# The last microseconds of a decode block: result columns split 304/208 between ScalarE and VectorE, and the last row's weight loads in front of its waiting matmul

## Chip, core and metric

One core of a Trainium2 chip. The metric is the device time of one execution in microseconds. A profile gives a span that is shorter than the time of the execution it was taken in (398.6 us for one of 401.14). The repeats and the experiments ran in groups on the chips numbered 3, 13 and 15; a ratio compares only executions of one group.

## The reference

One decode step. Attention with a cache of 65,536 keys in 4 groups of heads, and an MLP, added into one row of 1024 values. Only the ends matter here:

```python
return x + _A_ref(xn, A_k_cache, A_v_cache, A_wq, A_wo) + _B_ref(xn, B_w1, B_w2, B_w3, B_w4)
# _A_ref ends with      ... .reshape(B, Sq, Hq * Dh) @ wo
# _B_ref ends with      x1 + _gelu(_layernorm(x1, axis=-1) @ w3) @ w4        w4: 3584 x 1024
```

## The kernel before

All weights and the cache (170 MB) stream through three 8 MB buffers on one DMA queue. The last weight, w4, arrives in pieces of 8, 11, 5, 2 and 1 row blocks (of 128 rows each; a 28th block comes in small transfers and is computed earlier). "Row" below is such a block: 128 inputs times 1024 outputs. Rows 19 to 26 are computed "narrow": four 32-column tiles of the TensorE array work side by side, each on a quarter of the 1024 outputs. Quarters 0 and 1 go to one tile in PSUM, the memory that TensorE's results go to (half h = 0), 2 and 3 to another (h = 1). ScalarE copies the first half out, VectorE the second.

```python
W4_PIECES = (8, 11, 5, 2, 1)
WHOLE = 27
NARROW = 8
# ... all that comes before the tail is cut
    quarters = [ps_M.tile([P, 512], F32, name="pm_r", tag="pm") for _ in range(2)]
    sums = [ogpool.tile([64, 256], F32, name="sums_a", tag="og"), ppool.tile([64, 256], F32, name="sums_b", tag="p")]
    # ... inject(h, ...) is a matmul into quarters[h][64*h : 64*h+64, 0:256]; cut
    nc.scalar.copy(out=sums[0][:], in_=psB[0:64, 0:256])             # sums of the rows done so far
    nc.vector.tensor_copy(out=sums[1][:], in_=psB[0:64, 256:512])

    def narrow_rows(lo, hi):
        wt = st.tiles["w4"]
        for c in range(lo, hi):
            for h in range(2):
                for j in range(2):
                    q = 2 * h + j
                    nc.tensor.matmul(quarters[h][32 * q:32 * q + 32, 0:256], lhsT=hT[:, c:c + 1].to_broadcast([P, 32]),
                                     rhs=wt[:, D * c + 512 * j + 256 * h:D * c + 512 * j + 256 * (h + 1)], ...)

    with tc.issue_after(inject(0, ident_f[0:64, 0:64], sums[0][:], False)):   # half 0: old sums by TensorE
        narrow_rows(WHOLE - NARROW, WHOLE)

    out_t = ogpool.tile([64, 2, 256], BF16, name="out_t", tag="og")
    nc.scalar.copy(out=out_t[:, 0, :], in_=quarters[0][0:64, 0:256])
    nc.vector.tensor_tensor(out=out_t[:, 1, :], in0=quarters[1][64:128, 0:256], in1=sums[1][:], op=ALU.add)
    nc.scalar.dma_start(out=out[0, 0, :].rearrange("(j n) -> j n", j=2), in_=...)   # the store, from ScalarE's queue
```

Of the kernel before, what the change touches and what calls it, by code (L numbers as in the profile page):

```python
# [8 lines left out]
BF16 = mybir.dt.bfloat16  # L9
F32 = mybir.dt.float32  # L10
ACTF = mybir.ActivationFunctionType
ALU = mybir.AluOpType
# [3 lines left out]
P = 128  # L16
# [7 lines left out]
WHOLE = 27  # L24
FIRST = 6
NARROW = 8


def keep_loaded_weights(nc):




    for function in nc.m.functions:
        for block in function.blocks:
            held, kept = {}, []
            pe = [i for i in block.instructions if i.engine == mybir.EngineType.PE]
            user = dict(zip((i.name for i in pe), pe[1:]))
            for i in block.instructions:
                if i.engine == mybir.EngineType.PE:  # L40
                    if i.opcode == "Ldweights":
                        what = (i.tile_size, str(i.ins[0]))
                        waits = [j for j in (i, user[i.name]) if j.sync_info is not None and j.sync_info.on_wait]
                        if waits:
                            held.clear()
                        elif held.get(i.tile_position) == what and i.sync_info is None:
                            continue
                        if any(size != i.tile_size for size, _ in held.values()):
                            held.clear()
                        held[i.tile_position] = what  # L50
                    elif i.opcode != "Matmult" or i.ldweights is not False:
                        held.clear()
                kept.append(i)
            block.instructions = kept


# [41 lines left out]
def kernel(  # L98
# [13 lines left out]
):  # L112
    nc = tc.nc
    nc.at_finalize(keep_loaded_weights)
    nc.at_finalize(lead_with_the_first_load)
    nc.at_finalize(close_on_the_store)
    D = A_x.shape[-1]
# [19 lines left out]
    ppool = ctx.enter_context(tc.tile_pool(name="psb", bufs=1))  # L137
    ogpool = ctx.enter_context(tc.tile_pool(name="og", bufs=2))
# [82 lines left out]
    for b in range(2):  # L221
        nc.gpsimd.tensor_copy(
            out=spread[:, 2 * b:2 * b + 2, :].rearrange("p r (a i) -> p r a i", a=4),
            in_=ident_f[:, 64 * b:64 * b + 64].rearrange("p (i r) -> p r i", r=2).unsqueeze(2).to_broadcast([P, 2, 4, 32]))
# [8 lines left out]
    psB = ps_B.tile([P, 512], F32, name="psB")  # L233
# [6 lines left out]
    for a in range(4):  # L240
        nc.vector.transpose(out=x_t[32 * a:32 * a + 32].rearrange("p c j -> p (c j)"),  # L241
                            in_=x_row[:, 256 * a:256 * (a + 1)].rearrange("p (i c) -> p c i", c=DC))
# [3 lines left out]
    def layernorm(src, tag):  # L246
# [39 lines left out]
                          in_=sel8[:].unsqueeze(2).to_broadcast([P, 8, 16]))  # L286
# [49 lines left out]
    hT = const.tile([P, WHOLE + LEFT], BF16, name="hT")  # L336
# [119 lines left out]
    tail = {}  # L456
# [41 lines left out]
    def compute_w4(lo, hi):  # L498
# [3 lines that stand above are left out]
                mm = row_acc(j, hT[:, c:c + 1], wt[:, D * c + 512 * j:D * c + 512 * (j + 1)])  # L502
        return mm.ins
# [24 lines left out]
    with tc.issue_after(filled):  # L528
        projected = project(HKV - 1)
    quarters = [ps_M.tile([P, 512], F32, name="pm_r", tag="pm") for _ in range(2)]  # L530
    sums = [ogpool.tile([64, 256], F32, name="sums_a", tag="og"), ppool.tile([64, 256], F32, name="sums_b", tag="p")]
    pick = small.tile([64, 2, 32], F32, name="pick", tag="msk")
    nc.vector.tensor_copy(out=pick[:], in_=ident_f[0:64, 0:64].rearrange("p (j r) -> p j r", r=32)[:, :, 0:1].to_broadcast([64, 2, 32]))

    def inject(h, lhsT, rows, start):
        return nc.tensor.matmul(quarters[h][64 * h:64 * h + 64, 0:256], lhsT=lhsT, rhs=rows, start=start,
                                stop=False, tile_position=(0, 64 * h), skip_group_check=True).ins

    with tc.issue_after(projected):
        for h in range(2):  # L540
            begun = inject(h, pick[:].rearrange("p j r -> p (j r)"), tail["o"][0:64, 256 * h:256 * (h + 1)], True)
    with tc.issue_after(begun):
        compute_w4(early, WHOLE - NARROW)
    nc.scalar.copy(out=sums[0][:], in_=psB[0:64, 0:256])
    nc.vector.tensor_copy(out=sums[1][:], in_=psB[0:64, 256:512])

    def narrow_rows(lo, hi):
        wt = st.tiles["w4"]
        for c in range(lo, hi):
            for h in range(2):  # L550
                for j in range(2):
                    q = 2 * h + j
                    nc.tensor.matmul(quarters[h][32 * q:32 * q + 32, 0:256], lhsT=hT[:, c:c + 1].to_broadcast([P, 32]),
                                     rhs=wt[:, D * c + 512 * j + 256 * h:D * c + 512 * j + 256 * (h + 1)], start=False, stop=False,
                                     tile_position=(0, 32 * q), skip_group_check=True)

    with tc.issue_after(inject(0, ident_f[0:64, 0:64], sums[0][:], False)):
        narrow_rows(WHOLE - NARROW, WHOLE)

    out_t = ogpool.tile([64, 2, 256], BF16, name="out_t", tag="og")  # L560
    nc.scalar.copy(out=out_t[:, 0, :], in_=quarters[0][0:64, 0:256])
    nc.vector.tensor_tensor(out=out_t[:, 1, :], in0=quarters[1][64:128, 0:256], in1=sums[1][:], op=ALU.add)
    nc.scalar.dma_start(out=out[0, 0, :].rearrange("(j n) -> j n", j=2),
                        in_=out_t[31:33].rearrange("p h n -> p (h n)"))

# [1 line left out]
_INS = ['A_x', 'A_k_cache', 'A_v_cache', 'A_wq', 'A_wo', 'B_x', 'B_w1', 'B_w2', 'B_w3', 'B_w4']  # L567
# [26 lines left out]
```

## Time and profile before

| | before |
|---|---|
| time, first three executions | 400.79, 400.72, 401.16 us |
| profiled span | 398.6 us |
| last weight landed | 396.45 us |
| from there to the end of the span | 2.166 us |
| store issued, before the end of the span | 1.256 us |

The lines of the profile are shown and read in the prediction. In these lines PE is TensorE, PEld its weight loads, DVE VectorE, ACT ScalarE and ACTq ScalarE's queue; L553 is a line of the kernel, and the brackets give the engine's idle time before the instruction and what ended it.

### The profile page before, as it was taken

Reading aid. Unit: us, or ns where it says so; the run is one execution under the profiler, and the core shown is the slowest. Engines: PE = TensorE matmul, PEld = TensorE weight load, DVE = VectorE, ACT = ScalarE, POOL = GpSimd, SP = SyncE. Lnnn points to the kernel's source line nnn. Section 1 sums busy time; section 2 is a strip of 40 time slices with the busy share of each in tenths; the row PEclk is TensorE's granted clock in tenths of the full one; section 3 lists DMA queues with packets and bytes.
Section 4 is the critical chain, followed back from the end, with each engine's and each line's share of the span. In section 5 each row is a group of like instructions: output and inputs, shape, how many; then the busy total and the mean of one; then the engine's idle time right before and its main releaser. Section 6 shows DMA issues by size and latency. Waiting matters only on the chain.

```text
span 398.6 us, 2623 instructions
## 1 busy us (share of the span) xinstructions
PE 230.2 (58%) x1372; PEld 45.2 (11%) x862; DVE 211.5 (53%) x162; ACT 27.8 (7%) x36; POOL 10.0 (3%) x38
## 2 busy tenths in 40 slices
PE   0272970591569247834964297429553946394986
PEld 0210010000200010011001100101010102010142
DVE  0602010965196559643963696269449932894141
ACT  1002010003000200020002000200110020002000
POOL 2100000000000000000000000000000000002000
PEclk9998896697659686966895679678966986599999
DMA  9998999999999999999999999999999999999996
GB/s 421 421 443 382 439 441 480 434 427 421 416 428 427 434 460 442 427 427 421 427 429 427 467 434 434 423 421 427 441 429 441 454 427 388 418 455 431 409 427 260
DMA packets 4310, 170.03 MB, mean 427 GB/s; under 512 B 457, under 2 KB 459, under 8 KB 844
## 3 DMA queue, kind: packets, MB, share of 16 engines
q1 hardware_dynamic: 4294, 169.87, 98.9%
q8 instruction: 9, 0.15, 0.2%
q14 instruction: 1, 0.01, 0.0%
q10 hardware_dynamic: 6, 0.00, 0.0%
HBM read 169.87 MB, written 0.00 MB: 426 GB/s over the span
## 4 chain that ended last, share of the span: by engine, by line
DMA 54%; DVE 21%; PE 18%; ACT 2%; another core or an unknown queue 2%; SPq 1%; POOLq 1%; issue 1%; DVEq 0%; ACTq 0%
DMA big<-in_A_k_cache_dram 41%; DVE big L387 15%; PE sc L392 11%; DMA big<-in_B_w_dram 7%; DMA big<-in_A_wq_dram 6%; PE oacc L442 4%; DVE p_sb L413 2%; DVE mx L397 2%; PE psq L307 2%; ACT p_sb L410 2%; SPq L194 1%; POOLq L589 1%; ACT L410 0%; PE pm_mx L399 0%
## 5 line engine op out<-in xcount | busy, mean ns | idle before, releaser
L392 PE MATMUL sc<-big,qdiag 128*128 128x512 bf16 x512 | 128.5, 411 | 65.8 <-DVE big L387 65.6
L387 DVE STREAM_TRANSPOSE big<-big 128x4096 f32<-128x4096 f32 x32 | 139.4, 4412 | 48.0 <-DMA big<-in_A_k_cache_dram 48.0
L442 PE MATMUL oacc<-big,p_sb 128*32 128x512 bf16 x512 | 44.0, 520 | 34.5 <-DVE p_sb L413 34.5
L397 DVE TENSOR_REDUCE mx<-sc 128x1 f32<-128x2048 f32 x8 | 18.3, 2291 | 29.7 <-PE sc L392 29.7
L392 PEld LDWEIGHTS <-qdiag 128*128 128x128 bf16 x128 | 13.1, 102 | 176.6 <-issue 145.2
L410 ACT ACTIVATE p_sb<-sc,nball 128x2048 bf16<-128x2048 f32 x8 | 15.7, 1967 | 219.4 <-DVE nball L408 219.4
L413 DVE STREAM_TRANSPOSE p_sb<-p_sb 128x2048 bf16<-128x2048 bf16 x8 | 18.5, 2311 | 18.0 <-ACT p_sb L410 18.0
L442 PEld LDWEIGHTS <-p_sb 128*32 128x32 bf16 x512 | 16.8, 126 | 59.1 <-DVE p_sb L413 35.1
L451 DVE SCALAR_TENSOR_TENSOR og<-oacc,wb,og 128x512 f32<-128x512 f32 x4 | 3.0, 750 | 28.7 <-PE oacc L442 28.7
L307 PE MATMUL psh<-big,ln_rep_b 128*32 128x512 bf16 (+1 forms) x64 | 12.4, 942 | 4.0 <-DMA big<-in_B_w_dram 4.0
L485 PE MATMUL o_acc<-big,oT 128*1 128x512 bf16 x48 | 11.9, 413 | 2.4 <-ACT p_sb L410 2.4
L399 PE MATMUL pm_mx<-ident_f,mx 128*1 128x128 f32 x8 | 2.3, 283 | 19.1 <-DVE mx L397 19.1
L307 PE MATMUL psq<-big,ln_rep_a 128*32 128x512 bf16 x64 | 8.9, 445 | 4.1 <-DMA big<-in_A_wq_dram 4.1
L348 DVE STREAM_TRANSPOSE h_row<-h_row 128x896 bf16<-128x896 bf16 x1 | 1.1, 1111 | 17.2 <-ACT h_row L347 17.2
L332 POOL COPY qdiag<-qx 32x32 bf16<-32x32 bf16 x16 | 3.2, 203 | 262.8 <-PE sc L392 246.0
L250 PE MATMUL pm_ln<-ln_rowsum_a,ones_f 128*128 128x1 f32 x2 | 0.6, 348 | 12.5 <-DVE ln_rowsum_a L248 12.5
L320 DVE CAST q_row<-psq 64x1024 bf16<-64x1024 f32 x1 | 1.2, 1217 | 11.9 <-PE psq L307 11.9
L236 PE MATMUL psB<-big,hT 128*32 128x512 bf16 x46 | 5.5, 380 | 2.6 <-DMA big<-in_B_w_dram 2.6
L241 DVE STREAM_TRANSPOSE x_t<-x_row 32x256 bf16<-32x256 bf16 x4 | 2.5, 615 | 8.1 <-DMA x_row<-in_A_x_dram 8.0
L464 PE MATMUL pm_e<-ol,sel8big 128*128 128x129 f32 x6 | 1.8, 385 | 7.9 <-DVE ol L462 7.9
L406 PE MATMUL pm_mx<-ident_f,rep 1*128 1x1 f32 x8 | 1.9, 234 | 5.0 <-DVE rep L403 5.0
L448 ACT COPY og<-oacc 128x512 f32<-128x512 f32 x4 | 2.3, 585 | 33.5 <-PE oacc L442 24.4
(112 smaller groups left out, 77.1 us busy)
## 6 DMA issues: line engine op xcount, KB each, us to landing
big<-in_A_wo_dram SPq DMA_DIRECT2D x1, 8192.0 KB
big<-in_B_w_dram SPq DMA_DIRECT2D x1, 7168.0 KB
big<-in_B_w_dram SPq DMA_DIRECT2D x3, 2048.0 KB
big<-in_B_w_dram SPq DMA_DIRECT2D x1, 2816.0 KB
big<-in_B_w_dram SPq DMA_DIRECT2D x1, 1280.0 KB
big<-in_B_w_dram SPq DMA_DIRECT2D x1, 512.0 KB
big<-in_B_w_dram SPq DMA_DIRECT2D x1, 256.0 KB
big<-in_A_k_cache_dram SPq DMA_DIRECT2D x8
```

The source lines that it names most:

```text
L194: go(out=t[i0:i0 + 4 * k:4, WHOLE * D:(WHOLE + m) * D].rearrange("e (i n) -> e i n", i=m), in_=w4_v[m0:m0 + k * m, WHOLE, :].rearrange("(i ...
L236: return nc.tensor.matmul(psB[32 * j:32 * j + 32, :], lhsT=lhsT.to_broadcast([lhsT.shape[0], 32]), rhs=rhs, start=start, stop=False, tile_ ...
L307: nc.tensor.matmul(acc[32 * q:32 * q + 32, i, 0:n], lhsT=rep[:, c, :], rhs=cols(c, i, q), start=(c == 0), stop=(c == DC - 1), tile_positio ...
L332: nc.gpsimd.tensor_copy(out=qdiag[at, LEAD:].rearrange("p (x c) -> p x c", x=4)[:, :, 32 * a:32 * a + 8], in_=qx[at, :, 8 * g:8 * g + 8])
L387: nc.vector.transpose(out=words, in_=words)
L392: nc.tensor.matmul(sc[:, e, :], lhsT=qdiag[:, c0:c0 + P], rhs=cols[:, s, e, :, b2, :, r], start=(s == 0 and b2 == 0 and r == 0), stop=(s = ...
L397: nc.vector.reduce_max(out=mx[:], in_=sc[:].rearrange("p e n -> p (e n)"), axis=AX.X)
L410: nc.scalar.activation(out=p_sb[:], in_=sc[:], func=ACTF.Exp, bias=nball[:, b:b + 1], scale=SCALE, accum_out=group["lall"][:, b:b + 1])
L413: nc.vector.transpose(out=flat, in_=flat)
L442: mm = nc.tensor.matmul(oacc[32 * q:32 * (q + 1), :], lhsT=pT[:, e, 32 * t:32 * (t + 1)], rhs=vt[:, :, e, t, :], start=(e == 0 and t < 4), ...
L485: nc.tensor.matmul(tail["rows"][0:1, h2, :], lhsT=oT[g][:, j:j + 1], rhs=wt[:, g, j, 512 * h2:512 * (h2 + 1)], start=(g == 0 and j == 0), ...
L589: with _tile.TileContext(nc) as tc:
```

## The change

The intent: in the profile before, ScalarE is faster per column (0.83 against 1.04 ns) and starts 44 ns sooner than VectorE, so it takes more of the result columns (304 against 208); and the weights of the last row, which do not depend on the late transfer, are loaded before TensorE waits for that transfer.

```diff
+CUT = (0, 304, 512)
+def load_last_row_ahead(nc):
+    # (core of it) the last eight PE instructions are four pairs of load and matmul:
+            row = pe[-8:]
+            loads, sums = row[::2], row[1::2]
+            moved = {i.name for i in loads[1:]}
+            for i in block.instructions:
+                if i.name == sums[0].name:
+                    kept += loads[1:]          # in front of the matmul that waits
+                if i.name not in moved:
+                    kept.append(i)
-    sums = [... [64, 256] ..., ... [64, 256] ...]
+    cuts = [slice(CUT[h], CUT[h + 1]) for h in range(2)]
+    sums = [... [64, CUT[1]] ..., ... [64, CUT[2] - CUT[1]] ...]
-                    nc.tensor.matmul(quarters[h][32 * q:32 * q + 32, 0:256], ...
-                                     rhs=wt[:, D * c + 512 * j + 256 * h:D * c + 512 * j + 256 * (h + 1)], ...
+                    nc.tensor.matmul(quarters[h][32 * q:32 * q + 32, cuts[h]], ...
+                                     rhs=wt[:, D * c + 512 * j + CUT[h]:D * c + 512 * j + CUT[h + 1]], ...
-    nc.scalar.copy(out=out_t[:, 0, :], in_=quarters[0][0:64, 0:256])
-    nc.vector.tensor_tensor(out=out_t[:, 1, :], in0=quarters[1][64:128, 0:256], in1=sums[1][:], op=ALU.add)
+    nc.scalar.copy(out=out_t[:, cuts[0]], in_=quarters[0][0:64, cuts[0]])
+    nc.vector.tensor_tensor(out=out_t[:, cuts[1]], in0=quarters[1][64:128, cuts[1]], in1=sums[1][:], op=ALU.add)
```

(The injections and the copies out of psB take the same cuts.)

More of the change, by code (lines that the diff above doesn't have):

```diff
@@ L53, in keep_loaded_weights @@
                 kept.append(i)
+            block.instructions = kept
+def load_last_row_ahead(nc):
+    for function in nc.m.functions:
+        for block in function.blocks:
+            pe = [i for i in block.instructions if i.engine == mybir.EngineType.PE and i.opcode in ("Ldweights", "Matmult")]
+            if len(pe) < 8:
+                continue
+            row = pe[-8:]
+            loads, sums = row[::2], row[1::2]
+            assert all(i.opcode == "Ldweights" and i.sync_info is None for i in loads)
+            assert all(i.opcode == "Matmult" and i.tile_size == (P, 32) for i in sums)
+            assert sorted(i.tile_position for i in loads) == [(0, 32 * q) for q in range(4)]
+            moved = {i.name for i in loads[1:]}
+            kept = []
+            for i in block.instructions:
[3 more added lines that the diff above has]
+                    kept.append(i)
             block.instructions = kept
@@ L114 @@
     nc.at_finalize(keep_loaded_weights)
+    nc.at_finalize(load_last_row_ahead)
     nc.at_finalize(lead_with_the_first_load)
@@ L530 @@
     quarters = [ps_M.tile([P, 512], F32, name="pm_r", tag="pm") for _ in range(2)]
-    sums = [ogpool.tile([64, 256], F32, name="sums_a", tag="og"), ppool.tile([64, 256], F32, name="sums_b", tag="p")]
+    cuts = [slice(CUT[h], CUT[h + 1]) for h in range(2)]
+    sums = [ogpool.tile([64, CUT[1]], F32, name="sums_a", tag="og"),
+            ppool.tile([64, CUT[2] - CUT[1]], F32, name="sums_b", tag="p")]
     pick = small.tile([64, 2, 32], F32, name="pick", tag="msk")
@@ L535, in inject @@
     def inject(h, lhsT, rows, start):
-        return nc.tensor.matmul(quarters[h][64 * h:64 * h + 64, 0:256], lhsT=lhsT, rhs=rows, start=start,
+        return nc.tensor.matmul(quarters[h][64 * h:64 * h + 64, cuts[h]], lhsT=lhsT, rhs=rows, start=start,
                                 stop=False, tile_position=(0, 64 * h), skip_group_check=True).ins
@@ L540 @@
         for h in range(2):
-            begun = inject(h, pick[:].rearrange("p j r -> p (j r)"), tail["o"][0:64, 256 * h:256 * (h + 1)], True)
+            begun = inject(h, pick[:].rearrange("p j r -> p (j r)"), tail["o"][0:64, cuts[h]], True)
     with tc.issue_after(begun):
         compute_w4(early, WHOLE - NARROW)
-    nc.scalar.copy(out=sums[0][:], in_=psB[0:64, 0:256])
-    nc.vector.tensor_copy(out=sums[1][:], in_=psB[0:64, 256:512])
+    nc.scalar.copy(out=sums[0][:], in_=psB[0:64, cuts[0]])
+    nc.vector.tensor_copy(out=sums[1][:], in_=psB[0:64, cuts[1]])
     def narrow_rows(lo, hi):
@@ L552, in narrow_rows @@
                     q = 2 * h + j
-                    nc.tensor.matmul(quarters[h][32 * q:32 * q + 32, 0:256], lhsT=hT[:, c:c + 1].to_broadcast([P, 32]),
-                                     rhs=wt[:, D * c + 512 * j + 256 * h:D * c + 512 * j + 256 * (h + 1)], start=False, stop=False,
+                    nc.tensor.matmul(quarters[h][32 * q:32 * q + 32, cuts[h]], lhsT=hT[:, c:c + 1].to_broadcast([P, 32]),
+                                     rhs=wt[:, D * c + 512 * j + CUT[h]:D * c + 512 * j + CUT[h + 1]], start=False, stop=False,
                                      tile_position=(0, 32 * q), skip_group_check=True)
@@ L558 @@
         narrow_rows(WHOLE - NARROW, WHOLE)
-    out_t = ogpool.tile([64, 2, 256], BF16, name="out_t", tag="og")
-    nc.scalar.copy(out=out_t[:, 0, :], in_=quarters[0][0:64, 0:256])
-    nc.vector.tensor_tensor(out=out_t[:, 1, :], in0=quarters[1][64:128, 0:256], in1=sums[1][:], op=ALU.add)
-    nc.scalar.dma_start(out=out[0, 0, :].rearrange("(j n) -> j n", j=2),
-                        in_=out_t[31:33].rearrange("p h n -> p (h n)"))
+    out_t = ogpool.tile([64, 512], BF16, name="out_t", tag="og")
+    nc.scalar.copy(out=out_t[:, cuts[0]], in_=quarters[0][0:64, cuts[0]])
+    nc.vector.tensor_tensor(out=out_t[:, cuts[1]], in0=quarters[1][64:128, cuts[1]], in1=sums[1][:], op=ALU.add)
+    nc.scalar.dma_start(out=out[0, 0, :].rearrange("(j n) -> j n", j=2), in_=out_t[31:33, :])
 _INS = ['A_x', 'A_k_cache', 'A_v_cache', 'A_wq', 'A_wo', 'B_x', 'B_w1', 'B_w2', 'B_w3', 'B_w4']
```

## The prediction

> **What bounds the kernel now.** I read the page from the top: the DMA rows first, then the chain that ended last, then the end of the timeline, because the diff touches nothing but the last stage.
>
> ```profile
> DMA  9998999999999999999999999999999999999996
> q1 hardware_dynamic: 4294, 169.87, 98.9%
> HBM read 169.87 MB, written 0.00 MB: 426 GB/s over the span
> ```
>
> The DMA row is at nine tenths in nearly every slice and only its last slice drops to six. One load queue keeps the 16 engines at 98.9% of the span. So the kernel is a stream of 169.87 MB with compute beside it; nothing done on an engine shortens it, except after the last byte. The chain of waits in order of time says the same of the end:
>
> ```profile
> 384.40 12.05 DMA big<-in_B_w_dram
> 396.45 0.04 issue
> 396.50 0.34 PE pm_r L553 x4
> 396.84 0.02 issue
> 396.86 0.42 DVE out_t L562
> ```
>
> The last piece of w4 (one row of 128) lands at 396.45 us. What follows until the span's end at 398.6 us is 2.15 us, and that is all that an engine change can shorten. The timeline of this stretch shows who does what there:
>
> ```profile
> 394.10 0.36 ACT L544 COPY sums_a<-psB 64x256 f32<-64x256 f32 x1 [26.32 <-PE psB L236]
> 394.50 0.42 DVE L545 COPY sums_b<-psB 64x256 f32<-64x256 f32 x1 [5.08 <-ACT sums_a L544]
> 394.52 0.64 PE L536 MATMUL pm_r<-sums_a,ident_f 64*64 64x256 f32 x2 [0.46 <-ACT sums_a L544]
> 395.09 1.18 PE L553 MATMUL pm_r<-big,hT 128*32 128x256 bf16 x28
> 395.87 0.20 PEld L553 LDWEIGHTS <-hT 128*32 128x32 bf16 x8 [0.23 <-issue]
> 396.50 0.29 PE L553 MATMUL pm_r<-big,hT 128*32 128x256 bf16 x4 [0.23 <-DMA big<-in_B_w_dram]
> 396.50 0.10 PEld L553 LDWEIGHTS <-hT 128*32 128x32 bf16 x3 [0.43 <-issue]
> 396.82 0.36 ACT L561 CAST out_t<-pm_r 64x256 bf16<-64x256 f32 x1 [2.35 <-PE pm_r L553]
> 396.86 0.42 DVE L562 TENSOR_TENSOR out_t<-pm_r,sums_b 64x256 bf16<-64x256 f32 x1 [1.95 <-PE pm_r L553]
> 397.36 0.26 ACTq L563 DMA_DIRECT2D out_dram<-out_t  x1
> ```
>
> Four things to see. Of the last row's four weight loads only the first runs before the wait; three are recorded after the landing, among the matmuls. ScalarE starts 44 ns before VectorE (unrounded 396.817 and 396.861). ScalarE also finishes first (365 against 425 ns): 397.182 against 397.286. The store is issued at 397.362, 76 ns after VectorE, and the remaining 1.24 us to the span's end is the store's own.
>
> The trace's semaphore records give this in ns from the start of the last row (its first matmul, t = 0, 43 ns after the landing): second matmul done at 300, ScalarE from 322 to 687, fourth matmul done at 342, VectorE from 366 to 791, store issued at 867. The second and fourth signals lie 42 ns apart, so each matmul with its load follows the one before by 21 ns, and the first was done near 279.
>
> **What the Trainium skill says.** "TensorE: Matmul & The Clock Gate", section "Single matmul latency", gives (398 + N)/2.4 ns for a warm isolated matmul: 272 ns for N = 256. My 279 agrees within 7 ns; the granted clock was 1.00 from 396.0 to 397.4 us. The same page, section "The mechanism" with its list of what overlaps, says that a weight load runs beside matmuls in flight only when their row group differs, and that packed tiles otherwise start about 4 ns apart. All four tiles here span the same 128 rows, so the in-line loads should cost; the 21 ns spacing fits this. "PSUM — Partial Sum Buffer", "PSUM bank collisions raise a hardware error", asks that two engines keep to different banks or quadrants. The trace shows ScalarE and VectorE reading the result side by side, while the copies out of psB, one bank, are serial (394.10, then 394.50). The result halves already are two full-bank tiles before the change, so the words "banks of their own" describe no new overlap. "ScalarE: Activation LUTs", "What ACT_TABLE_LOAD costs", gives 0.833 ns per column; the trace agrees: a 64x1024 cast from PSUM took 1003 ns, (1003 - 365)/768 = 0.831.
>
> **The change part by part.** The instruction order of both builds differs in the last eight PE instructions only (four loads, then four matmuls, instead of pairs) and in the widths. Counts are the same: no instruction, transfer or wait goes or comes.
>
> *Widths at the end.* ScalarE takes 304 columns: 365 + 48 x 0.831 = 405 ns. VectorE takes 208: its slope from PSUM is (1217 - 416)/768 = 1.043 ns per column (64x1024 cast against the 64x256 copy), so 425 - 50 = 375 ns. The matmuls of the first half get 48 columns more, 48/2.4 = 20 ns; those of the second half 20 ns less.
>
> *Loads ahead.* The three later loads move into idle time of PE. If spacing falls from 21 to about 4 ns, the matmuls end like this: first 279 + 20 = 299, second 303; the fourth would be done by 279 - 20 + 12 = 271 by itself, but matmuls end in order, so about 303 to 311.
>
> *Sum.* ScalarE starts 22 ns after its signal, at 325, and ends at 730. VectorE starts 24 ns after, at 327 to 335, and ends at 702 to 710. The later end is now 730 instead of 791, so 61 ns are gained. The store followed the late engine by 76 ns, of which 38 were the queue's separate wait for VectorE. That wait now ends early and only ScalarE's remains, which may save up to 36 ns more. Together 61 to 97 ns; I take 70. The landing, the row's start and the store's 1.24 us stay.
>
> *Earlier in the tail.* The copy of psB to sums_a grows by 40 ns, and the two-pass f32 injection of 304 columns by about 2 x 50 ns (its two passes start 260 ns apart for 256 columns, 1.02 ns per column). So rows 19 to 23 start near 395.23 instead of 395.09. The last of them was issued at 395.55, and PE then waited for the next piece until 395.87: 0.32 us of slack, of which 0.14 is used, plus some 20 ns for width. It is hidden. VectorE's copy of sums_b starts 40 ns later, shrinks by 50, and has nearly 2 us to spare.
>
> **The rivals.**
> (1) *The loads cost nothing*, because the queue hides them already or the spacing is the matmuls' own. Then only the widths act: second matmul done at 300 + 20 = 320, fourth near 322, ScalarE 342 to 747, VectorE 346 to 721. End 747 against 791: 44 ns. For it: the reported load and matmul starts lie 1 to 2 ns apart. Against it: the 42 ns between the two signals. Time 400.75.
> (2) *ScalarE becomes too late*: 304 columns overshoot if the loads were the whole delay of VectorE. With loads alone (256/256) the end would be at about 279 + 12 + 24 + 425 = 740, so the widths add only 10 ns to that. It is still no loss: ScalarE would have to start after 386 to end later than 791. Time 400.75 to 400.80.
> (3) *The longer injection delays the rows until a landed piece waits for PE.* For it: the slack shrinks from 0.32 to some 0.16 us. Against it: two more waits for DMA follow, the last with 0.23 us of idle PE. A landing some 0.2 us earlier in another execution would use it up, and even then only part reaches the end. Time at most 400.9.
> (4) *The stream moves more than the tail.* The three timed runs go from 400.72 to 401.16 and the profiled execution took 401.14. This scatter, 0.44 us, is six times my gain. It decides what is measured, and I expect no separable difference from few rounds.
>
> **Range and chances.** 400.79 - 0.07 = 400.72 us, 0.02% less. The mechanism leaves 0 to 0.1 us of gain; the scatter of the stream, of the same size on either side of this value as among the four executions and a little for another chip, sets the range: 400.25 to 401.25. Two per cent would be 8 us, almost four times the whole 2.15 us after the last landing, so faster by that is excluded unless the stream changed. Slower by that would need a stall that nothing here offers. Within 2%: 0.99.
>
> **What would show it right or wrong.** In the changed kernel's profile: ScalarE's last cast near 405 ns and VectorE's last sum near 375; their starts within some 15 ns of each other instead of 44; the store issued about 0.80 us after the start of the last row instead of 0.867, and still 1.24 us before the span's end; three loads gone from behind the last landing; rows 19 to 23 starting near 395.23 and still waiting for the next piece. Starts still 25 ns or more apart would mean that the loads were not the spacing. A span that differs by more than 0.1 us with the same tail after the landing means that the stream moved, not the change. The prediction is wrong if the row's start no longer follows the landing by 43 ns, which would mean that four loads in a row hold the matmul up.

## The result

The changed kernel took 400.51 us (median of 6 executions, 400.45 to 400.76); the kernel before 400.81 (6 executions, 400.72 to 401.16). The ratio is 0.9993 with a 95% interval of 0.998 to 1.0006: the same. (A ratio here is the mean time of one kernel's runs over that of the other's in the same rounds, so it is not quite the ratio of the medians.) The predicted 400.72 us is 0.21 us off, inside its range. But the measured difference of 0.3 us is four times the 0.07 us predicted, so the first question is whether 0.3 us is real.

The DMA rows of the changed kernel's page:

```profile
DMA  9998999999999999999999999999999998999996
q1 hardware_dynamic: 4294, 169.87, 99.0%
HBM read 169.87 MB, written 0.00 MB: 426 GB/s over the span
```

The stream is the same in bytes and rate. The end of the chain of waits, in order of time:

```profile
384.19 12.15 DMA big<-in_B_w_dram
396.34 0.04 issue
396.38 0.34 PE pm_r L578 x2
396.72 0.02 issue
396.74 0.38 DVE out_t L587
```

The last piece landed at 396.34 us instead of 396.45: 0.11 of the 0.17 us by which the span is shorter (398.618 to 398.450) lie ahead of anything that the change does in the tail. From landing to end it is 2.113 us against 2.166: 53 ns. The timeline of the tail, in the same form as in the prediction:

```profile
393.99 0.41 ACT L569 COPY sums_a<-psB 64x304 f32<-64x304 f32 x1 [26.42 <-PE psB L259]
394.42 0.37 DVE L570 COPY sums_b<-psB 64x208 f32<-64x208 f32 x1 [4.33 <-ACT sums_a L569]
394.44 0.72 PE L561 MATMUL pm_r<-sums_a,ident_f 64*64 64x304 f32 x2 [0.49 <-ACT sums_a L569]
395.10 0.90 PEld L578 LDWEIGHTS <-hT 128*32 128x32 bf16 x32 [0.47 <-issue]
395.10 1.09 PE L578 MATMUL pm_r<-big,hT 128*32 128x304 bf16 x28
396.38 0.29 PE L578 MATMUL pm_r<-big,hT 128*32 128x304 bf16 x4 [0.19 <-DMA big<-in_B_w_dram]
396.71 0.41 ACT L586 CAST out_t<-pm_r 64x304 bf16<-64x304 f32 x1 [2.32 <-PE pm_r L578]
396.74 0.38 DVE L587 TENSOR_TENSOR out_t<-pm_r,sums_b 64x208 bf16<-64x208 f32 x1 [1.95 <-PE pm_r L578]
397.20 0.26 ACTq L588 DMA_DIRECT2D out_dram<-out_t  x1
```

The line of three weight loads behind the landing is gone; all 32 loads are one group that ends at 396.00. (The timeline names a merged group by its first shape: the x28 and x4 hold both widths.) ScalarE's cast grew to 406 ns, VectorE's sum shrank to 377. But the two engines still start 35 ns apart, not within 15, and VectorE still ends last.

From here on all times of the tail are in ns from the start of the last row (its first matmul, 41 to 43 ns after the last landing in every run), read from the trace's instruction and semaphore records. "Signal" is the semaphore update by which a matmul tells an engine that its half is done: by the second matmul for ScalarE, by the fourth for VectorE.

| run | first signal | second signal | ScalarE | VectorE | store | landing to end, us |
|---|---|---|---|---|---|---|
| before | 300 | 342 | 322-687 | 366-791 | 867 | 2.166 |
| changed | 308 | 342 | 331-737 | 366-743 | 819 | 2.113 |

The store comes 48 ns sooner, exactly what VectorE's sum lost in length (425 - 377). The second signal did not move at all, where the prediction had it move from 342 to between 303 and 311.

### The profile page after: what moved, and what is told of

The parts are those of the page before. It is cut to its first block, busy times and chain, and to the rows that moved or that the text cites. A ratio compares the mean times of both kernels' runs of the same rounds, so it can differ in the third digit from the quotient of the medians.

```text
span 398.4 us, 2623 instructions
## 1 busy us (share of the span) xinstructions
PE 234.3 (59%) x1372; PEld 45.1 (11%) x862; DVE 211.4 (53%) x162; ACT 27.9 (7%) x36; POOL 10.1 (3%) x38
## 4 chain that ended last, share of the span: by engine, by line
DMA 54%; DVE 21%; PE 18%; ACT 2%; another core or an unknown queue 2%; SPq 1%; POOLq 1%; issue 1%; DVEq 0%; ACTq 0%
DMA big<-in_A_k_cache_dram 41%; DVE big L410 15%; PE sc L415 11%; DMA big<-in_B_w_dram 8%; DMA big<-in_A_wq_dram 5%; PE oacc L465 4%; PE psq L330 2%; DVE p_sb L436 2%; DVE mx L420 2%; ACT p_sb L433 2%; SPq L217 1%; POOLq L613 1%; ACT L433 0%; DVE m L424 0%
## 5 line engine op out<-in xcount | busy, mean ns | idle before, releaser
L415 PE MATMUL sc<-big,qdiag 128*128 128x512 bf16 x512 | 130.7, 417 | 63.8 <-DVE big L410 63.8
L508 PE MATMUL o_acc<-big,oT 128*1 128x512 bf16 x48 | 13.0, 440 | 2.4 <-ACT p_sb L433 2.4
L330 PE MATMUL psq<-big,ln_rep_a 128*32 128x512 bf16 x64 | 9.9, 486 | 3.9 <-DMA big<-in_A_wq_dram 3.9
```

The costliest lines, as they stand in the source:

```text
L330: nc.tensor.matmul(acc[32 * q:32 * q + 32, i, 0:n], lhsT=rep[:, c, :], rhs=cols(c, i, q), start=(c == 0), stop=(c == DC - 1), tile_positio ...
L415: nc.tensor.matmul(sc[:, e, :], lhsT=qdiag[:, c0:c0 + P], rhs=cols[:, s, e, :, b2, :, r], start=(s == 0 and b2 == 0 and r == 0), stop=(s = ...
L508: nc.tensor.matmul(tail["rows"][0:1, h2, :], lhsT=oT[g][:, j:j + 1], rhs=wt[:, g, j, 512 * h2:512 * (h2 + 1)], start=(g == 0 and j == 0), ...
```

## The experiments

Three theories of the 42 ns between the two signals were on the table: A, the predicted one (the loads between the matmuls space them by 21 ns); B, it is mostly a cost of having a second signal; C, the loads cost nothing. All kernels below gave a correct result.

### The two kernels again

Both files unchanged, timed against the kernel before.

> The kernel before, unchanged, timed against itself: it gives the scatter that every other verdict has to beat, and a second look at its tail. All theories: ratio 1.000 with an interval of about +-0.001; in ns from the start of the last row, first signal (second matmul) near 300, second signal (fourth matmul) near 342, VectorE 366 to 791, store issued at 867, each within 10 ns of the first profile. If the timed gap of 0.3 us between the two kernels is scatter of the stream, a difference of 0.1 to 0.3 us can show up here too.

> The changed kernel again. If only the tail is shorter (53 ns from the last landing to the end in the first profiles), the ratio is 0.9999 and not separable from 1; if the change really takes 0.3 us, the ratio is 0.9993 again and its interval lies below the one of the kernel before against itself. Tail in ns from the start of the last row: signals at 308 and 342, ScalarE 331 to 737, VectorE 366 to 743, store issued at 819, each within 10 ns.

> The changed kernel a third time, on the same chip as the run beside it: tail again with signals at 308 and 342 and the store at 819 within 3 ns; ratio to the kernel before between 0.999 and 1.001, its interval including 1.

| run | signals | ScalarE | VectorE | store | landed at, us | landing to end, us | ratio (interval) |
|---|---|---|---|---|---|---|---|
| before again | 300, 342 | 323-689 | 366-791 | 867 | 396.40 | 2.158 | 0.9999 (0.9987 to 1.0012) |
| changed, 2nd | 308, 342 | 331-736 | 366-743 | 820 | 396.21 | 2.116 | 1.0003 (0.9990 to 1.0017) |
| changed, 3rd | 308, 342 | 330-735 | 365-742 | 818 | 396.74 | 2.111 | 0.9993 (0.9979 to 1.0006) |

The tail repeats within 2 ns up to the store, so one profile suffices to judge it. The time does not: the 0.3 us of the first rounds were gone in the second (1.0003) and back in the third. The landing of the last piece went from 396.21 to 396.74 us over the three profiles of one and the same kernel. Each interval of the changed kernel includes 1. Putting the three sets together (16 executions, mean 400.71 us, against 24 of the kernel before, mean 400.89) leaves a lean of 0.18 us, with a standard error near 0.07 from the scatter of 0.19 to 0.23 us of one execution; set by set the difference of the means is -0.29, +0.05 and -0.25 us. The 0.05 us of the tail is in that lean; whether there is more in it, these runs do not settle.

### One part of the change at a time

Loads ahead alone, with halves of 256:

```diff
-CUT = (0, 304, 512)
+CUT = (0, 256, 512)
```

> Loads in front of the waiting matmul, halves of 256 and 256 as before. Theory A (in-line loads space the matmuls by 21 ns, as predicted): signals near 283 and 291, VectorE ends near 740, store issued near 816. Theory B (the gap between the two signals belongs to the signals, some 34 ns at least, and the loads cost only about 12 ns before the first one): signals near 288 and 322, VectorE ends near 771, store near 847. Theory C (loads cost nothing): signals at 300 and 342, store at 867, as in the kernel before. Time: within 0.1 us of the kernel before in all three.

Widths alone, loads left in pairs:

```diff
-    nc.at_finalize(load_last_row_ahead)
```

> Halves of 304 and 208, the last row's loads in their pairs as before. Theory A: signals near 320 and 342 or a little less, ScalarE the last to end near 748, store near 800 to 824. Theory B: signals near 320 and 354, VectorE ends near 755, store near 831. Theory C: the same as the changed kernel, signals at 308 and 342, VectorE ends at 743, store at 819. Time: within 0.1 us of the kernel before in all three.

| run | signals | ScalarE | VectorE | store | landing to end, us | ratio (interval) |
|---|---|---|---|---|---|---|
| loads alone | 288, 322 | 311-676 | 345-771 | 848 | 2.135 | 1.0001 (0.9988 to 1.0013) |
| widths alone | 320, 363 | 344-749 | 387-762 | 839 | 2.138 | 0.9998 (0.9985 to 1.0010) |

The timelines, first with loads alone, then with widths alone:

```profile
395.93 0.12 PEld L578 LDWEIGHTS <-hT 128*32 128x32 bf16 x4
396.45 0.27 PE L578 MATMUL pm_r<-big,hT 128*32 128x256 bf16 x4 [0.22 <-DMA big<-in_B_w_dram]
396.76 0.36 ACT L586 CAST out_t<-pm_r 64x256 bf16<-64x256 f32 x1 [2.32 <-PE pm_r L578]
396.79 0.43 DVE L587 TENSOR_TENSOR out_t<-pm_r,sums_b 64x256 bf16<-64x256 f32 x1 [1.90 <-PE pm_r L578]
397.30 0.26 ACTq L588 DMA_DIRECT2D out_dram<-out_t  x1
```

```profile
396.40 0.31 PE L577 MATMUL pm_r<-big,hT 128*32 128x304 bf16 x4 [0.20 <-DMA big<-in_B_w_dram]
396.40 0.10 PEld L577 LDWEIGHTS <-hT 128*32 128x32 bf16 x3 [0.40 <-issue]
396.74 0.41 ACT L585 CAST out_t<-pm_r 64x304 bf16<-64x304 f32 x1 [2.33 <-PE pm_r L577]
396.79 0.38 DVE L586 TENSOR_TENSOR out_t<-pm_r,sums_b 64x208 bf16<-64x208 f32 x1 [1.97 <-PE pm_r L577]
397.24 0.27 ACTq L587 DMA_DIRECT2D out_dram<-out_t  x1
```

In the first, the four loads stand at 395.93, half a microsecond before the matmuls at 396.45; in the second, three are behind the landing again. Loads ahead move the first signal by 12 ns and the second by 20. The widths move both by 20 to 21 ns the other way, although the fourth matmul itself became shorter: the second signal cannot overtake the first. The two parts add up: 300 - 12 + 20 = 308, and 342 - 20 + 21 = 343, where 342 was measured. Theory B met the loads-alone run to the ns (288 and 322); A and C fall. For the widths alone B was 9 ns short at the second signal (354 expected, 363 measured), because it had left out the 8 ns that the two later loads cost.

### What the remaining gap is made of

With loads ahead the gap is still 34 ns. Either every matmul is done 17 ns after the one before (B2), or the second signal costs the gap (B1). One signal in place of two; ScalarE waits for the fourth matmul as VectorE does, which is safe:

```diff
+    nc.at_finalize(signal_once)    # second matmul: no update; fourth: adds both amounts;
+                                   # ScalarE's wait: the value that VectorE waits for
```

> The changed kernel with one signal in place of two: the second matmul of the last row signals nothing, ScalarE waits for the fourth as VectorE does. Theory B1 (the 34 ns gap is a cost of the second signal): the one signal comes near 308 to 315 ns after the row's start, VectorE ends near 712, ScalarE near 740, store near 816. Theory B2 (each matmul is done some 17 ns after the one before, signal or not): the one signal comes at 342, ScalarE ends near 769, store near 845.

And the order of the last row changed, so that the third and the fourth matmul signal:

```diff
-            for h in range(2):
-                for j in range(2):
-                    q = 2 * h + j
+            for q in ((0, 2, 1, 3) if c == WHOLE - 1 else (0, 1, 2, 3)):
+                for h, j in (divmod(q, 2),):
```

> The changed kernel with the last row's matmuls in the order first half, second half, first half, second half, so that the third and fourth signal instead of the second and fourth. B1 (cost of a second signal): signals near 310 and 344, still 34 apart. B2 (a step of 17 ns for each matmul): signals near 325 and 342, 17 apart, and ScalarE ends near 752, store near 829. Under neither theory is it faster than the changed kernel.

| run | signals | ScalarE | VectorE | store | landing to end, us |
|---|---|---|---|---|---|
| one signal | 316 (4th matmul) | 338-743 | 339-716 | 792 | 2.090 |
| interleaved | 311, 341 (3rd, 4th) | 334-740 | 365-742 | 818 | 2.112 |

The timeline with one signal:

```profile
396.35 0.29 PE L606 MATMUL pm_r<-big,hT 128*32 128x304 bf16 x4 [0.20 <-DMA big<-in_B_w_dram]
396.69 0.41 ACT L614 CAST out_t<-pm_r 64x304 bf16<-64x304 f32 x1 [2.34 <-PE pm_r L606]
396.69 0.38 DVE L615 TENSOR_TENSOR out_t<-pm_r,sums_b 64x208 bf16<-64x208 f32 x1 [1.94 <-PE pm_r L606]
397.14 0.27 ACTq L616 DMA_DIRECT2D out_dram<-out_t  x1
```

Both engines now start at 396.69. Without the second matmul's signal the fourth one's comes 26 ns sooner (342 to 316), so that signal was what held it. The fourth matmul's signal alone comes 8 ns later than the second's did (308 to 316), 4 ns per matmul, and in the interleaved row the gap is 30 = 4 + 26. So the 42 ns of the kernel before are 2 x 4 for the matmuls, 8 for the two loads between them and 26 for the second signal. B1 holds. The interleaved row is the cross-check: it moves both signals by 3 ns or less (308 to 311, 342 to 341) and the store by 1 ns. Both runs were profiled once and not timed in rounds. One expectation failed: with one signal the store was to come at 816, 76 ns after ScalarE, and came at 792, 76 ns after VectorE, though ScalarE ended 27 ns later than VectorE (743 against 716). What the store waits for is taken up below.

The Trainium skill has this: "TensorE: Matmul & The Clock Gate", section "The cost: per-tile semaphore tail", says that increments serialise and gives 4.7 ns per tile and 26.3 ns per increment. The 4 and 26 ns here agree. The prediction used other sections of that page and passed this one by.

### Better versions

If the second signal is late anyway, the engine with the longer way to the store should have the first one. VectorE's half first, loads ahead, and new cuts:

```diff
+            for q in ((2, 3, 0, 1) if c == WHOLE - 1 else (0, 1, 2, 3)):
-CUT = (0, 304, 512)
+CUT = (0, 272, 512)
```

> Meant as a better version: the last row does VectorE's half first, with halves of 272 (ScalarE) and 240 (VectorE) columns, loads in front. First signal 308 - 64/2.4 = 281, second 34 later = 315 if the gap stays (both theories agree). VectorE 305 to 713 (425 - 16 x 1.04 = 408), ScalarE 337 to 715 (365 + 16 x 0.83 = 378), store near 791 against 819 of the changed kernel. Time: 0.03 us less than the changed kernel, not separable by timing.

The other way is one signal with cuts for equal starts:

```diff
+    nc.at_finalize(signal_once)
-CUT = (0, 304, 512)
+CUT = (0, 288, 512)
```

> One signal as in the first run of this call, with halves of 288 and 224 that balance equal starts. B1: signal near 301 to 308, both engines end near 718 to 725, store near 796 to 802. B2: signal near 335, both end near 751, store near 828. Time: within 0.1 us of the kernel before.

VectorE's half first with 288 and 224:

```diff
-CUT = (0, 272, 512)
+CUT = (0, 288, 512)
```

> VectorE's half first again, now with 288 and 224 columns. Ground: the store followed VectorE's end by 76 to 77 ns where VectorE was last, but ScalarE's end by only 49 ns in the run with one signal, where the wait for VectorE had long been met; so ScalarE, which issues the store, should end some 28 ns after VectorE. Reckoned: signals at 274 and 309, VectorE 297 to 690, ScalarE 331 to 722, store near 770 (819 in the changed kernel, 867 before). If the 49 ns were an accident of that run, the store comes 76 ns after ScalarE, near 798. Time: 0.05 us under the changed kernel, not separable by timing.

The next two cuts, (0, 336, 512) and (0, 296, 512), ask what ScalarE's own end costs:

> In every run so far the store followed VectorE's end by 76 to 77 ns, also where ScalarE ended later (743 and 722 against a store at 792 and 766), so ScalarE's end has bound nothing yet, and the ground given for the run before was wrong. This run makes ScalarE late on purpose: VectorE's half first, 336 and 176 columns. Reckoned: signals near 254 and 329, VectorE 277 to 621, ScalarE 351 to 783. If only VectorE's end counted, the store would come at 698, before its data are there, which the wait forbids; so it shows the true distance from ScalarE's end to the store: near 0 to 15 ns (the queue waits for nothing else), near 44 to 49 (as far as seen), or 76 (the same as for VectorE).

> One step beyond 288: 296 and 216 columns, VectorE's half first. Signals near 271 and 312, VectorE 293 to 678, ScalarE 334 to 732. If ScalarE's end binds only at some 20 ns or less before the store, the store comes at 755, 11 ns sooner than with 288; if it needs 44, at 776, 10 ns later. Time: not separable from the other variants.

| run | signals | ScalarE | VectorE | store | landing to end, us | ratio (interval) |
|---|---|---|---|---|---|---|
| VectorE first, 272 | 281, 315 | 337-715 | 303-712 | 789 | 2.089 | 0.9993 (0.9977 to 1.0010) |
| one signal, 288 | 309 | 332-724 | 332-726 | 802 | 2.104 | 0.9995 (0.9981 to 1.0010) |
| VectorE first, 288 | 274, 308 | 330-722 | 296-689 | 766 | 2.060 | 0.9995 (0.9982 to 1.0007) |
| VectorE first, 296 | 270, 307 | 330-729 | 293-677 | 759 | 2.060 | 1.0003 (0.9986 to 1.0019) |
| VectorE first, 336 | 255, 324 | 347-779 | 279-622 | 809 | 2.107 | one run only |

The tail of the version with 288, and of the one with 336:

```profile
396.31 0.29 PE L577 MATMUL pm_r<-big,hT 128*32 128x224 bf16 x4 [0.22 <-DMA big<-in_B_w_dram]
396.61 0.39 DVE L586 TENSOR_TENSOR out_t<-pm_r,sums_b 64x224 bf16<-64x224 f32 x1 [1.90 <-PE pm_r L577]
396.64 0.39 ACT L585 CAST out_t<-pm_r 64x288 bf16<-64x288 f32 x1 [2.34 <-PE pm_r L577]
397.07 0.26 ACTq L587 DMA_DIRECT2D out_dram<-out_t  x1
```

```profile
396.80 0.34 DVE L586 TENSOR_TENSOR out_t<-pm_r,sums_b 64x176 bf16<-64x176 f32 x1 [1.87 <-PE pm_r L577]
396.86 0.43 ACT L585 CAST out_t<-pm_r 64x336 bf16<-64x336 f32 x1 [2.31 <-PE pm_r L577]
397.33 0.27 ACTq L587 DMA_DIRECT2D out_dram<-out_t  x1
```

In both, VectorE now starts first (396.61 before 396.64, 396.80 before 396.86).

The cost of the second signal is not simply added on. With loads ahead and one half computed after the other, the gap is 34 ns for equal halves, and also where the second half is narrower (changed kernel) or little wider (272 and 288). With 296 and 336 columns it is 37 and 69 ns, and there the 80 and 160 columns that the second half has more account for nearly all of it: an estimate from the widths-alone run, where 48 columns moved the first signal by 20 ns, gives 33 and 67 ns. So the later matmuls run on while the first signal is under way. A second half that is wider costs nothing here as long as its extra columns fit into the gap.

The ground that I gave for 288 was wrong. There the store still came 77 ns after VectorE (689 to 766), as in every other run where ScalarE was not very late, though ScalarE ended 33 ns later. With 336, where ScalarE ends 157 ns after VectorE, ScalarE clearly binds, and the store follows it by 30 ns (779 to 809). So the store comes at the later of VectorE's end + 77 and ScalarE's end + 30. (None of the distances expected before that run, 0 to 15, 44 to 49 or 76, was right.) The records of ScalarE's queue show the two waits one after the other. In the kernel before, the wait for VectorE is over at 829, 38 ns after VectorE's end, and the store follows 38 ns after that. With 336 that wait is over at 659, ScalarE's own signal comes at 788, and the store 21 ns after it. The run with 296 has both nearly in balance: 729 + 30 = 759, the measured time, and 677 + 77 is 5 ns less; there too the store follows ScalarE's signal by 21 ns. VectorE's half first with 288 or 296 has the shortest tail of all, 2.060 us from landing to end: 53 ns less than the changed kernel and 106 ns less than the one before. In time it cannot be told from either (0.9995 and 1.0003).

## Why the prediction was right, and where it was not

**The bound: right.** The stream sets the time; the change can act on the tail alone. The tail became 53 ns shorter (2.166 to 2.113 us). The scatter (0.44 us predicted, up to 0.77 us within one set of executions of one kernel) decided what was measured, as the fourth rival said: the same changed file gave ratios of 0.9993, 1.0003 and 0.9993.

**Durations of the two engines: right.** 405 and 375 ns were predicted, 406 and 377 measured.

**Width of the first half: right.** It was to delay ScalarE's signal by 20 ns, and the widths alone moved it from 300 to 320.

**Width of the second half, and the loads: the step that was wrong.** The prediction took the 42 ns between the signals as 2 x 21 ns of spacing by in-line loads, and let loads ahead take it down to about 4 ns per matmul, so 51 ns at the second signal (342 to 291 for equal halves). The runs show 20 ns there (322), of which 12 are already in the first signal. The other term, 26 ns for the second of two signals, was missing from the sum; it was still there with the loads ahead. The prediction had read the 21 ns as agreeing with the skill's sentence that weight loads run beside matmuls in flight only where their row groups differ. The trace of the kernel before does not bear that out: the three later loads are recorded as starting 1, 5 and 8 ns after the row's first matmul, beside matmuls in flight on the same 128 rows (in other columns), and all three together cost 20 ns.

**Which engine ends last: wrong, as a result.** ScalarE was to end last at 730 with VectorE at 702 to 710; measured were 737 and 743. The 61 to 97 ns became 48. That this is of the predicted size is in part luck, for it was reached by another path: at the second signal the loads' gain (20 ns) and the widths' cost (21 ns) cancel, and the 48 ns are the shortening of VectorE's sum alone. Of the predicted sum the first 61 counted on VectorE starting at 327 to 335 (it stayed at 366). The extra 36 counted on the wait for VectorE being over early (with VectorE last it never was; the run with 336 shows that such a saving exists, 30 ns in place of 76). The own check in the prediction caught it: "Starts still 25 ns or more apart would mean that the loads were not the spacing", and they were 35 apart. The sign that it named for its being wrong as a whole, a row's start that no longer follows the landing by 43 ns, did not show (41 ns). Two of its readings were off by rounding: the store's own part is 1.256 us and not 1.24, the stretch after the landing 2.166 and not 2.15.

**The first rival came near for the wrong reason.** It gave 44 ns, with loads that cost nothing, signals at 320 and 322, and ScalarE last. The loads do cost 12 to 20 ns, and VectorE is last. The second rival, ScalarE too late, did not come about: ScalarE ends 6 ns before VectorE.

**The earlier part of the tail: hidden as predicted, but with no margin.** From ScalarE's copy to row 19 it took 1.11 us instead of 0.99, so 0.12 against the 0.14 predicted. But the slack was reckoned from the start of row 23's last matmul. Counted from when a tile is free for the next row, 109 ns after its matmul of row 23 started, it was 0.22 us before the change, not 0.32. And the widths cost 20 ns in each of five rows, 0.10 in all, not 20 ns once. Together 0.22 us: the slack is gone. The trace shows it. In all six runs with 304 columns the 304-column matmuls of row 24 start 655 or 656 ns after the start of row 19, which is 129 ns after those of row 23, whether their piece landed at 587 or at 613: they wait for the tile as long as for the piece, or longer. With equal halves row 24 starts 42 ns after its piece landed. So the condition of the third rival was met in part. It does no harm because the last piece lands some 0.6 us after that one, with room for the two rows between.

**"Banks of their own"** (words that the prediction quotes about the change)**: right that nothing new comes of it.** ScalarE and VectorE read the two halves side by side in both kernels (322-687 and 366-791 before, 331-737 and 366-743 after).

## What to carry to other kernels

When a kernel is a stream with a tail, judge a change to the tail by the profile, from the last landing to the end: it repeated within some 10 ns (within 2 ns up to the store), where single executions of one kernel lay up to 770 ns apart. Split a gap between two completion signals into matmuls, loads and the signals themselves before you optimise one of them; here the second signal was the largest part (26 of 42 ns). Here it paid to give the first signal to the engine whose end was farther from the next step (VectorE, 77 ns), and the longer piece, computed second, to the engine that issues that step itself (ScalarE, 30 ns).

## What the Trainium skill lacked or had wrong

- "TensorE: Matmul & The Clock Gate", section "The cost: per-tile semaphore tail": right in size (4 ns per matmul and 26 ns per signal here: 316 with one signal, 308 and 342 with two). What its sum does not say is that the cost of a signal is not added where later matmuls are wider: with 176 columns first and 336 second the signals are 69 ns apart, of which the extra columns account for an estimated 67.
- The same page, section "The mechanism", says that matmuls are in program order in start and end. For tiles of unequal width the recorded starts are not: in the changed kernel, from the start of row 19, the 208-column matmuls of rows 19 to 23 begin at 6, 105, 195, 284 and 373 ns and the 304-column ones at 0, 139, 268, 397 and 526, so those of row 23 begin before the wider ones of row 22. The completion signals stayed in order (with one signal the 208-column fourth matmul's comes at 316, after the 308 of the 304-column second one).
- The same page, section "LDWEIGHTS (loading the stationary operand)", gives columns/1.2 ns for a weight load, by which 32 columns would take an estimated 27 ns. What such loads cost between matmuls of neighbouring column tiles is not said there and is less here: 12 ns by the second matmul (one load) and 20 ns by the fourth (three).
- No page that I read gives the distance from an engine's end to a store on a queue: 76 to 77 ns after VectorE for a store on ScalarE's queue in all runs where VectorE's end set it, and 30 ns after ScalarE itself.
